# Attention in groups of 256 tokens, uneven FFN blocks and all weight casts on one engine, in a fused attention and FFN kernel

## The chip, the cores and the metric

The kernel runs on one core of one Trainium2 chip. The metric is the device time of one execution in microseconds (us), as the median of several executions. The profile is one execution recorded by the hardware profiler; its span is 1.7 to 2.1 us shorter than the time that is reported for it. Executions are called fast when they lie within 1.5% of the fastest of the same kernel, and only those are compared.

## The reference, cut to what matters

Attention within chunks of 64 tokens for 8 heads of 64, then a feed-forward network (FFN) with a squared Relu:

```python
# q, k, v: (8 batches, 8 heads, 576, 64) float32, each split into chunks of 64 tokens
scores = scale * q_c @ k_c.T
attn = exp(scores - max(scores)) / (sum(...) + 1e-09)
x = (attn @ v_c)                 # as 4608 tokens x 512
h = np.maximum(x @ w_in, 0.0)    # w_in: 512 x 2048
out = (h * h) @ w_out            # w_out: 2048 x 512, out: 4608 x 512 float32
```

## The kernel before

Tokens are handled in nine blocks of 512. The FFN of a block runs on TensorE, and the attention of the next block is laid between its matmuls. The scheduler keeps the program's own order, so the place of a call in the source is its place in each engine's queue. The parts that matter here:

```python
wst_pool = tile_pool(name="wst", bufs=2)          # staging of float32 weights
...
def load_w_in(i):
    ...
    for h in range(2):
        eng = nc.vector if h == 0 else nc.gpsimd  # half of the casts on VectorE
        eng.tensor_copy(out=w_in_bf[...], in_=st[...])
...
def transpose_qk(j, r):
    ps = ps_att.tile([128, 1024], FP32, name="ps_att")
    psb = ps.bitcast(BF16)                        # 2048 bf16 columns
    for which, src in ((0, q_sb), (1, k_sb)):
        ... 8 transposes of src into psb[:, which*1024 : (which+1)*1024]
    for which in range(2):                        # both copies after all 16
        nc.vector.tensor_copy(out=qkT[:, which], in_=psb[:, which * 1024:(which + 1) * 1024])
...
def ffn_in(j):
    for ft in range(n_ft):                        # 16 slices
        ... 4 matmuls into a ps_ffn tile h
        nc.scalar.activation(out=rl, in_=h, func=AF.Relu)
        nc.vector.tensor_tensor(out=gT[:, ft, :], in0=rl, in1=rl, op=ALU.mult)
...
o_sb = ffn_pool.tile([128, d_model], FP32, name="o_sb", bufs=4)   # output staging
```

The matmuls of the FFN therefore depend on two other engines: ScalarE does Relu and frees a ps_ffn tile, VectorE squares it. VectorE also does the copies of the attention.

Some names, for the lines below. Tiles called ps_* lie in PSUM, the memory that TensorE writes its results into; the other tiles lie in SBUF, the on-chip memory that holds inputs and weights. qkT is q and k transposed, xT the attention's result transposed (the input of the first FFN product), rl the Relu, gT its square (the input of the second FFN product), o_sb the output staging. GpSimd casts weights to bf16, SyncE issues the transfers (DMA). A semaphore is a counter that one engine raises and another waits for. In all fences `...` stands for lines that are left out.

The softmax here doesn't subtract the row's maximum and nothing guards it: scores larger than these inputs give would overflow.

## Time and profile before

| | before |
|---|---|
| time, median of 3 executions | 351.23 us |
| span of the profile | 349.6 us |
| first FFN matmul | 58.14 us |
| one block of 512 tokens with attention inside | 32.03 us |

The first 58 us are start-up, the rest is bound by TensorE; the prediction below shows the lines for that. One more line also belongs here, and I did not look at it before I predicted. It is a row of the page's list of costliest groups: line, engine, operation, tiles, count, then busy time and mean ns of one, then the idle time of the engine just before such instructions and who ended it.

```profile
L142 PE MATMUL ps_att<-ident,k_sb 128*128 128x128 bf16 x144 | 12.1, 229 | 0.2 <-DMA k_sb<-in_k_dram 0.2
```

Before all 144 transposes of k together TensorE stood idle for 0.2 us. They follow the transposes of q with nothing between them.

### The profile page before, as it was taken

The numbers are of one execution on the slowest core, as the hardware profiler recorded it, in microseconds if no ns is written. First come the engines' busy times: TensorE is split into PE (matmuls) and PEld (weight loads), VectorE is DVE, ScalarE is ACT, GpSimd is POOL, SyncE is SP. The second block draws the span as 40 slices with busy tenths as digits, with TensorE's granted clock in tenths as the row PEclk, the third lists the DMA queues.
The fourth block names the chain that finished last, engine by engine and source line by source line (L and its number), as shares of the span: only waits on it lengthen the run. The fifth ranks groups of instructions, "written<-read, shape, count | busy, mean of one in ns | idle before, by whom it ended". The sixth has DMA issues, their size and how long they took to land.

```text
span 349.6 us, 6592 instructions
## 1 busy us (share of the span) xinstructions
PE 293.8 (84%) x2693; PEld 149.9 (43%) x2736; DVE 132.1 (38%) x314; ACT 123.0 (35%) x199; POOL 11.6 (3%) x17
## 2 busy tenths in 40 slices
PE   0400026999999999999999999999999999999995
PEld 0300013454554555455445545554554455454442
DVE  0012136343465235615541652356155416522400
ACT  1000020542355137314722551473147225514621
POOL 1024220000000000000000000000000000000000
PEclk9999999999999999999999999999999999999999
DMA  9979689793397249427932971494289220011002
GB/s 173 175 264 348 224 233 181 169 200 80 110 220 134 83 125 198 104 86 162 171 93 80 223 144 68 127 194 104 90 173 175 77 83 9 3 60 62 0 39 81
DMA packets 123165, 46.56 MB, mean 133 GB/s; under 512 B 114432, under 2 KB 114432, under 8 KB 123136
## 3 DMA queue, kind: packets, MB, share of 16 engines
q1 hardware_dynamic: 123136, 46.15, 56.6%
q8 instruction: 21, 0.34, 0.5%
q14 instruction: 8, 0.07, 0.1%
HBM read 36.70 MB, written 9.44 MB: 132 GB/s over the span
## 4 chain that ended last, share of the span: by engine, by line
PE 82%; DMA 7%; SPq 5%; DVE 3%; issue 1%; ACT 0%; POOL 0%
PE ps_ffn L240 36%; PE ps_ffn L260 36%; DMA w_out_st<-in_moe_w_out_dram 5%; PE ps_att L142 4%; PE ps_att L211 3%; SPq L83 2%; DMA w_in_st<-in_moe_w_in_dram 2%; PE ps_att L182 2%; PE ps_att L162 2%; SPq L102 1%; SPq L95 1%; DVE w_out_bf L124 1%; DVE qkT L147 1%; DVE x L193 1%; POOL w_in_bf L114 0%
## 5 line engine op out<-in xcount | busy, mean ns | idle before, releaser
L240 PE MATMUL ps_ffn<-xT,w_in_bf 128*128 128x512 bf16 x552 | 131.8, 385 | 2.9 <-DVE xT L215 1.6
L260 PE MATMUL ps_ffn<-w_out_bf,gT 128*128 128x512 bf16 x557 | 129.1, 379 | 1.1 <-issue 0.2
L246 ACT ACTIVATE rl<-ps_ffn 128x512 bf16<-128x512 f32 x144 | 85.0, 600 | 59.8 <-PE ps_ffn L240 59.8
L247 DVE TENSOR_TENSOR gT<-rl 128x512 bf16<-128x512 bf16 x144 | 60.6, 425 | 95.7 <-ACT rl L246 92.7
L240 PEld LDWEIGHTS <-w_in_bf 128*128 128x128 bf16 x576 | 55.2, 99 | 65.2 <-issue 4.5
L260 PEld LDWEIGHTS <-gT 128*128 128x128 bf16 x576 | 54.8, 98 | 62.5 <-DVE qkT L147 0.3
L252 ACT COPY o_sb<-ps_ffn 128x512 f32<-128x512 f32 x36 | 20.8, 588 | 110.0 <-PE ps_ffn L260 106.7
L162 PE MATMUL ps_att<-qkT 64*64 64x64 bf16 x576 | 7.0, 199 | 35.0 <-DVE qkT L147 35.0
L169 ACT ACTIVATE e<-ps_att 128x1024 bf16<-128x1024 f32 x18 | 17.5, 1023 | 53.2 <-PE ps_att L162 53.2
L215 DVE COPY xT<-ps_att 128x1024 bf16<-128x1024 bf16 x18 | 12.5, 692 | 46.9 <-PE ps_att L211 46.9
L193 DVE TENSOR_TENSOR x<-ps_att,rec 128x256 bf16<-128x256 f32 x72 | 27.2, 419 | 1.2
L147 DVE COPY qkT<-ps_att 128x1024 bf16<-128x1024 bf16 x36 | 23.0, 683 | 1.8 <-PE ps_att L142 1.8
L162 PEld LDWEIGHTS <-qkT 64*64 64x64 bf16 x576 | 5.9, 112 | 38.8 <-DVE qkT L147 35.4
L142 PE MATMUL ps_att<-ident,q_sb 128*128 128x128 bf16 x144 | 12.4, 229 | 10.3 <-DMA q_sb<-in_q_dram 10.2
L142 PEld LDWEIGHTS <-q_sb 128*128 128x128 bf16 x144 | 9.9, 102 | 14.8 <-DMA q_sb<-in_q_dram 11.0
L114 DVE CAST w_in_bf<-w_in_st 128x1024 bf16<-128x1024 f32 x4 | 2.8, 694 | 29.9 <-DMA w_in_st<-in_moe_w_in_dram 29.9
L189 DVE RECIPROCAL rec<-ps_att 128x8 f32<-128x8 f32 x36 | 7.3, 201 | 13.4 <-PE ps_att L182 13.4
L142 PE MATMUL ps_att<-ident,k_sb 128*128 128x128 bf16 x144 | 12.1, 229 | 0.2 <-DMA k_sb<-in_k_dram 0.2
L211 PE MATMUL ps_att<-ident,x 128*128 128x128 bf16 x144 | 11.7, 229 | 0.5 <-DVE x L193 0.5
L211 PEld LDWEIGHTS <-x 128*128 128x128 bf16 x144 | 10.0, 103 | 4.5 <-DVE x L193 0.6
L182 PE MATMUL ps_att<-v_sb,e 64*64 64x65 bf16 x576 | 9.0, 201 | 2.3 <-DVE x L193 1.4
L182 PEld LDWEIGHTS <-e 64*64 64x64 bf16 x576 | 6.6, 111 | 9.5 <-issue 3.8
(13 smaller groups left out, 25.5 us busy)
## 6 DMA issues: line engine op xcount, KB each, us to landing
out_dram<-o_sb SPq DMA_DIRECT2D x36, 256.0 KB, 2.0
q_sb<-in_q_dram SPq DMA_DIRECT2D x32, 256.0 KB, 5.0
k_sb<-in_k_dram SPq DMA_DIRECT2D x32, 256.0 KB, 4.9
v_sb<-in_v_dram SPq DMA_DIRECT2D x80, 64.0 KB, 2.7
v_sb<-in_v_dram SPq DMA_DIRECT2D x32, 128.0 KB, 3.2
w_in_st<-in_moe_w_in_dram SPq DMA_DIRECT2D x4, 1024.0 KB, 5.3
w_out_st<-in_moe_w_out_dram SPq DMA_DIRECT2D x8, 512.0 KB, 4.1
q_sb<-in_q_dram SPq DMA_DIRECT2D x8, 128.0 KB, 4.0
```

Source lines behind the costliest of these rows:

```text
L142: nc.tensor.transpose(out=psb[:, c0:c0 + 128], in_=srcb[:, t, 2 * hp:2 * hp + 2, 1::2], identity=ident)
L147: nc.vector.tensor_copy(out=qkT[:, which], in_=psb[:, which * 1024:(which + 1) * 1024])
L162: nc.tensor.matmul(out=ps[64 * c:64 * c + 64, o0:o0 + 64], lhsT=qkT[64 * a:64 * a + 64, 1, hh, cols], rhs=qkT[64 * a:64 * a + 64, 0, hh, c ...
L169: nc.scalar.activation(out=e.rearrange("p a h t q -> p (a h t q)"), in_=ps, func=AF.Exp, scale=scale)
L182: nc.tensor.matmul(out=ps[64 * p:64 * p + 64, a, hp * (D + 1):(hp + 1) * (D + 1)], lhsT=e[64 * c:64 * c + 64, a, hp % 2, t, :], rhs=vb[64 ...
L193: nc.vector.tensor_tensor(out=x[:, :, a, :], in0=o[:, a, :, 0:D], in1=rec[:, a].to_broadcast([128, n_hp, D]), op=ALU.mult)
L211: nc.tensor.transpose(out=psb[:, c0:c0 + 128], in_=x[:, hp].rearrange("p a d -> p (a d)"), identity=ident)
L240: nc.tensor.matmul(out=h, lhsT=w_in_bf[:, dt, ft * 128:(ft + 1) * 128], rhs=xT[:, dt, :], start=(dt == 0), stop=(dt == n_dt - 1))
L246: nc.scalar.activation(out=rl, in_=h, func=AF.Relu)
L247: nc.vector.tensor_tensor(out=gT[:, ft, :], in0=rl, in1=rl, op=ALU.mult)
L252: nc.scalar.copy(out=o_sb, in_=o_ps)
L260: nc.tensor.matmul(out=o_ps, lhsT=gT[:, ft, tt * 128:(tt + 1) * 128], rhs=w_out_bf[:, ft, :], start=(ft == 0), stop=(ft == n_ft - 1))
```

## The change

The intent is to start the FFN much earlier. The attention is cut into 18 groups of 256 tokens, so that the first xT is ready sooner. VectorE is freed of the weight casts, which had stood ahead of its attention copies; all go to GpSimd. The first FFN block takes three groups (768 tokens), the last takes one (256), so that the start has more work to lay beside the weight loads and the end less to drain. Five staging buffers in place of two, one gT buffer in place of two. Cut to its core:

```diff
-    TCH = 512
+    GT = 256
+    blocks = [[0, 1, 2]] + [[g, g + 1] for g in range(3, n_grp - 1, 2)] + [[n_grp - 1]]
...
-    wst_pool = ctx.enter_context(tc.tile_pool(name="wst", bufs=2))
+    wst_pool = ctx.enter_context(tc.tile_pool(name="wst", bufs=5))
...
-            eng = nc.vector if h == 0 else nc.gpsimd
-            ... eng.tensor_copy(...)
+        nc.gpsimd.tensor_copy(out=w_in_bf[:, :, cols], in_=st)
...
-            for which, src in ((0, q_sb), (1, k_sb)):
-                ... 8 transposes
-            for which in range(2):
-                nc.vector.tensor_copy(
-                    out=qkT[:, which], in_=psb[:, which * 1024:(which + 1) * 1024])
+        for which in range(2):
+            ... 8 transposes
+            dst = qkT[:, which]
+            src = psb[:, which * 1024:(which + 1) * 1024].rearrange("c (h t) -> c h t", h=n_hp)
+            if which == 0:
+                nc.vector.tensor_copy(out=dst, in_=src)
+            else:
+                nc.scalar.copy(out=dst, in_=src)
...
+    load(0)
+    load(1)
+    load_w_in(0)
+    load_w_in(1)
+    load(2)
+    for i in range(2, 8):
+        load_w_in(i)
+    for i in range(8):
+        load_w_out(i)
```

The order of the loads and the slots at which attention is laid between the matmuls (a table called plan) change with it.

## The prediction

> **What bounds the kernel now.** I began with the page's busy shares and its row of tenths. Each slice is 8.74 us.
>
> ```profile
> PE 293.8 (84%) x2693; PEld 149.9 (43%) x2736; DVE 132.1 (38%) x314; ACT 123.0 (35%) x199; POOL 11.6 (3%) x17
> PE   0400026999999999999999999999999999999995
> POOL 1024220000000000000000000000000000000000
> DMA  9979689793397249427932971494289220011002
> ```
>
> TensorE is full from slice 7 to the end and does almost nothing in the first six: the kernel is a start-up of about 58 us and then a TensorE-bound stretch. DMA is busy from the start, but not the bound later. Next I read the timeline of the start.
>
> ```profile
> 12.60 0.40 PE L142 MATMUL ps_att<-ident,k_sb 128*128 128x128 bf16 x2 [0.15 <-DMA k_sb<-in_k_dram]
> ...
> 17.05 10.10 SPq L109 DMA_DIRECT2D w_in_st<-in_moe_w_in_dram  x4
> 22.57 0.69 DVE L114 CAST w_in_bf<-w_in_st 128x1024 bf16<-128x1024 f32 x1 [22.57 <-DMA w_in_st<-in_moe_w_in_dram]
> 22.60 1.56 POOL L114 CAST w_in_bf<-w_in_st 128x1024 bf16<-128x1024 f32 x1 [20.79 <-DMA w_in_st<-in_moe_w_in_dram]
> ...
> 34.69 1.04 POOL L124 CAST w_out_bf<-w_out_st 128x1024 bf16<-128x1024 f32 x1 [1.10 <-DMA w_out_st<-in_moe_w_out_dram]
> ...
> 47.21 0.69 DVE L124 CAST w_out_bf<-w_out_st 128x1024 bf16<-128x1024 f32 x1 [4.09 <-DMA w_out_st<-in_moe_w_out_dram]
> 47.82 2.48 DVE L147 COPY qkT<-ps_att 128x1024 bf16<-128x1024 bf16 x4
> 49.16 0.51 PEld L162 LDWEIGHTS <-qkT 64*64 64x64 bf16 x32 [34.72 <-DVE qkT L147]
> ...
> 58.14 0.59 PE L240 MATMUL ps_ffn<-xT,w_in_bf 128*128 128x512 bf16 x1 [0.78 <-DVE xT L215]
> ```
>
> q and k of the first 512 tokens are there at 12.6 us. Their transposes then lie in PSUM for 34.7 us, because VectorE takes its instructions in order and its share of the weight casts (the last at 47.21) stands ahead of the qkT copies. Those casts come slowly: each pair of staging buffers must be filled and cast before the next transfer is issued. The first FFN matmul is at 58.14.
>
> Last, the chain that ended last, for the price of a steady block and of the end.
>
> ```profile
> 126.22 1.73 PE ps_ffn L240 x8
> ...
> 158.25 1.73 PE ps_ffn L240 x8
> ...
> 318.50 6.69 PE ps_ffn L240 x31
> ...
> 346.16 0.59 ACT o_sb L252
> ```
>
> A block of 512 tokens with the next block's attention inside is 158.25 - 126.22 = 32.03 us. The last one, with none inside, is 346.16 - 318.50 = 27.66, that is 128 matmuls of 0.216 us. So attention of 512 tokens costs TensorE 4.37 us, of a group of 256 tokens 2.18. From 346.16 to the end of the span (349.6) the tail is 3.4 us. The steady part has no slack to give; only the first 58 us have.
>
> **What the Trainium skill says.** (1) "SBUF — State Buffer", section "Who interferes with whom": a VectorE instruction in a two-port mode, or one with two SBUF inputs, and a GpSimd instruction that reads SBUF exclude each other for a whole instruction. The trace agrees as far as it goes: the GpSimd cast that began 0.03 us after a VectorE cast took 1.56 us, the ones alone 1.04 (their access patterns differ too, so this is not proof). The product rl times rl (two SBUF inputs, 425 ns) should meet the casts in the same way. (2) "DMA: Bandwidth & Descriptors", section "Why small descriptors are slow (HBM only)": each packet carries a fixed overhead. Here the 256-byte rows of q, k, v moved at about 211 to 219 GB/s (4 to 13 us), the weights' 2 KB rows at up to 388 (27 to 32 us). (3) "TensorE: Matmul & The Clock Gate", section "What's actually happening": the array runs at half rate until it has been busy for a window of 3.4 us, and falls back after an idle one. In the trace the FFN's weight loads come every 0.43 us from 58.94 to 63.63 and then at 0.21: some 13 slow matmuls, costing 2.8 us once.
>
> **The change part by part.**
>
> *Queue order.* One queue (SyncE) issues every transfer in program order, and the instruction listing of the changed kernel gives: groups 0 and 1, two w_in chunks of 512 KB, group 2, six w_in chunks, eight w_out chunks, groups 3 and 4, groups 5 and 6, and only then the six stores of the first block. Before, 512 tokens of q, k, v took the queue from 0.74 to 17.05, so 8.2 us a group (later, between 46.4 and 65.4 and with more split transfers, 9.5; from 65.4 to 82.7, 8.7). I take 8.2 for groups 0 and 1, 9 for group 2 (split at a batch edge), 8.7 later.
>
> *First attention.* VectorE has no casts any more. Group 0's q and k land at about 7.8 us (before, one 256 KB transfer landed each 1.2 us from 4.21 on). Transposes to 8.7, the k copy now on ScalarE (1.02, as its 128x1024 exp) to 9.8, scores 1.3 at half clock, exp 1.02, values, reciprocal 0.2 and product, x transposes, xT copy 0.7: about 16. The product becomes one instruction of 128x512, estimated at 0.69 us from two of 0.419 less one fixed part of about 0.15. Group 1 follows it in program order, with its transposes at about 16 to 17.3, v landing near 20, the same chain, and xT ready at about 25. FFN starts at 25 instead of 58.1: 33 us sooner. w_in chunks 0 and 1, issued at 17 and 18, are cast by about 24.
>
> *First block, 768 tokens.* Four slices of ft for 512 tokens: 13 slow matmuls and 3 fast, 6.2 us, to 31.2; transposes of group 2, 0.9, to 32.1. w_in chunk 2 is issued after group 2, at about 27.6, lands at 31 and is cast at about 32.2, so there is almost no wait. Twelve further slices, 10.4, and the rest of group 2's attention, 1.9: 44.4. Then 64 matmuls of 256 columns at half of 0.216, 6.9; ScalarE's Relu at 256 columns is about 0.6 - 0.21 = 0.39 for each 0.43 of TensorE, so nearly level: to about 52. w_out: 14 casts of 1.04 (14.6) and the products meanwhile (12 of 0.425 and 16 of about 0.29, 9.7) share one port; 24.3 from 31.2 on is 55.5. The first output tile wants the last w_out chunk at 55, so I give this 1 us. Six output tiles of 16 x 0.216 = 3.45 make 20.7, attention of groups 3 and 4 another 4.4, the last xT copy 0.8: the second block could begin at about 80.
>
> *Stores.* Five staging buffers let w_out's last chunk be issued when the third w_out cast is done, about 46. Groups 3 and 4 take the queue to about 64, 5 and 6 to about 82. The first store lands near 84.5. There are only four o_sb buffers for six output tiles: the fifth copy on ScalarE waits for that store, and every Relu of the next block stands behind it. TensorE can fill the two other ps_ffn buffers (two slices, 1.73 us, to 81.7) and then waits to about 85. I count 3.3 us, so the second block in effect starts at 83.3.
>
> *Rest.* Six blocks of 32.03 (192.2), one with a single group inside (29.85), the last of 256 tokens (7 + 6.9 = 13.9), tail 3.4: 239.3. The single gT buffer costs nothing, since its first new write comes after the last old read in any case. The k copy adds 2 x 1.02 us of ScalarE to a block, into a half where Relu and exp (11.7 of about 17 us) leave room, with four ps_ffn buffers to cover it.
>
> Sum: 83.3 + 239.3 = 322.6 us of span. The span before was 349.6 where the time was 351.2, so 1.6 is added: **324 us**, 7.7% less. Cross-check: 33 us saved at the start, about 6 given back in waits, gives the same.
>
> **Rivals.** *A: no new wait.* If the queue issues faster (8.2 us a group throughout, 2 us less over four groups) or the stores land at once, the wait for o_sb nearly vanishes: 320 or a little under. For it: in the trace before a queue of 64 KB v transfers goes at a steady 0.6 us each, with few waits. Against it: DMA is at 90% and more in the first slices, and the loads between 46 and 65 us needed 9.5 us a group. *B: the first block becomes DMA- and queue-bound.* 10.5 MB of q, k, v and 8 MB of weights stand ahead of the first store. At 9.5 us a group for the last four the store would go out at 85; if the clock also falls back in the wait (3 us idle is near the window of the third skill item) that adds up to 3: 328 to 331. *C: casts become the bound.* If the port is held against GpSimd more than I take (say 2.2 us a cast), w_out is complete only at about 63, TensorE stands for 8 us at the first output tile, and everything behind slips: 331 to 334. For it: VectorE is busy all through this stage; against it: only two products fall into each 1.73 us. *D: the steady blocks lose*, for instance 0.3 us each through ScalarE, 2 us in all.
>
> **Range and chances.** The gain of 33 us at the start rests on one clear wait of 34.7 us, and none of the rivals returns more than about 12 of it. So A is the low end and B or C the high: 317 to 332. Faster by over 2% (under 344.2): 0.97; within 2%: 0.025; slower: 0.005.
>
> **What would show it.** The first FFN input matmul starting at 23 to 27 us; GpSimd casts of w_out of more than 1.04 us where products run; TensorE idle for 2 to 5 us at about 80 to 86 us with ScalarE's output copy waiting for a store's transfer; 32.0 us from block to block afterwards. I am wrong if FFN starts after 30, if TensorE waits for w_in slices or for w_out by more than 3 us, if no wait shows at the first stores, or if a steady block takes more than 32.3.

## The result, and the profile after

| | before | after |
|---|---|---|
| time, median of 4 executions each, same chip | 350.83 us | 352.54 us |
| lowest and highest | 350.21 to 351.24 | 352.24 to 353.04 |
| span of the profile | 349.6 us | 350.2 us |
| first FFN matmul | 58.14 us | 24.57 us |

The ratio is 1.0052, with a 95% interval of 1.0029 to 1.0075: the same within 2%, and if anything slower. Every ratio in this document is the mean time of one kernel's fast runs over that of the kernel before's fast runs in the same rounds, so it is not quite the ratio of the medians quoted. The output was correct here and in every experiment.

The FFN starts 33.6 us earlier, and the kernel ends no earlier. From the page of the changed kernel, the busy shares, then tenths of 8.76 us each:

```profile
PE 303.3 (87%) x2800; PEld 157.9 (45%) x2800; DVE 120.7 (34%) x268; ACT 142.7 (41%) x233; POOL 18.6 (5%) x28
...
PE   2456979989589988998899889988998899899995
POOL 1021681000000000000000000000000000000000
```

TensorE is now half busy in slice 3 and 70% busy or more from slice 5 on, but for slice 11 and the last. But it shows 8s to the end, in a pattern of two 9s and two 8s, where before it showed only 9s: about four slices are one block of 35 us, so every block has an idle part. The casts now lie in slices 3 to 7 of GpSimd. First the start, from the timeline (start, duration, engine, line, operation, tiles, count; in brackets the idle time before it and who ended it):

```profile
24.57 5.83 PE L224 MATMUL ps_ffn<-xT,w_in_bf 128*128 128x512 bf16 x16 [0.78 <-DVE xT L209]
...
34.84 4.27 PE L224 MATMUL ps_ffn<-xT,w_in_bf 128*128 128x512 bf16 x12 [2.07 <-POOL w_in_bf L113]
...
46.46 3.70 DVE L231 TENSOR_TENSOR gT<-rl 128x512 bf16<-128x512 bf16 x4
...
50.83 7.16 PE L224 MATMUL ps_ffn<-xT,w_in_bf 128*128 128x256 bf16 x64 [2.42 <-DVE xT L209]
```

The FFN starts as foreseen. At 34.84 it had waited 2.07 us for a w_in cast, and the next 12 matmuls took 4.27 us, 0.356 each, where 12 at 0.216 would take 2.59. At 50.83 it had waited 2.42 us for an xT copy on VectorE, which stood behind four products that took 0.9 us each. Next the chain that ended last (start, duration, what): the hand-over to the second block, and the block boundaries.

```profile
86.35 2.51 DMA out_dram<-o_sb
88.97 0.59 ACT o_sb L247
...
126.03 1.74 PE ps_ffn L224 x8
...
161.05 1.74 PE ps_ffn L224 x8
...
301.14 1.74 PE ps_ffn L224 x8
...
332.54 6.99 PE ps_ffn L224 x64
...
346.46 0.59 ACT o_sb L247
```

The wait for the stores came, as foreseen: the chain has the sixth output copy waiting for the second store. The fifth, at 88.17, came after 9.46 us without work on ScalarE; the profile puts its release down to TensorE, but in experiment 1 the same copy is put down to the first store. A block is now 161.05 - 126.03 = 35.02 us where it was 32.03. From 126.03 to 301.14 there are five of them, 175.1. The eighth block, with one group inside, is 332.54 - 301.14 = 31.40. The granted clock of TensorE is listed as 1.00 in the steady block before and after, so a lower clock is not the cause.

Where in a block do 3.0 us go? Of the page's list of costly groups, the row that answers to the one shown of before:

```profile
L139 PE MATMUL ps_att<-ident,k_sb 128*128 128x128 bf16 x144 | 12.2, 233 | 23.9 <-DVE qkT L146 23.9
```

The transposes of k do the same work in the same time, but TensorE now stands 23.9 us before them, all of it for the copy of q on VectorE (L146): 18 waits, one a group, the longest 3.5 us. The timeline of a steady block, just after its start at 126.03, shows one:

```profile
127.56 0.43 DVE L231 TENSOR_TENSOR gT<-rl 128x512 bf16<-128x512 bf16 x1 [5.12 <-ACT rl L230]
127.60 0.61 PE L139 MATMUL ps_att<-ident,q_sb 128*128 128x128 bf16 x8
127.80 0.60 ACT L230 ACTIVATE rl<-ps_ffn 128x512 bf16<-128x512 f32 x1 [0.27 <-PE ps_ffn L224]
...
128.43 0.43 DVE L231 TENSOR_TENSOR gT<-rl 128x512 bf16<-128x512 bf16 x1 [0.44 <-ACT rl L230]
...
128.77 0.69 DVE L146 COPY qkT<-ps_att 128x1024 bf16<-128x1024 bf16 x1
...
129.51 0.61 PE L139 MATMUL ps_att<-ident,k_sb 128*128 128x128 bf16 x8 [1.30 <-DVE qkT L146]
...
132.54 0.61 PE L139 MATMUL ps_att<-ident,q_sb 128*128 128x128 bf16 x8
...
134.51 0.61 PE L139 MATMUL ps_att<-ident,k_sb 128*128 128x128 bf16 x8 [1.36 <-DVE qkT L146]
```

Read it upwards from the line of 129.51. The k transposes wait 1.30 us for the q copy. The q copy could have run at 128.21, when the q transposes were done, but VectorE takes its instructions in order, and the product ahead of it had to wait until ScalarE's Relu ended at 128.40. So TensorE stands until Relu, a product and a copy have gone by. The second group of the block has the same wait, of 1.36 us (the last line).

Why must k wait for a copy of q, which lies in other columns? The program's instruction listing shows it. This is the first k transpose of the changed kernel, with the semaphores that it waits for, and the same instruction of the kernel before:

```
after   L139 Matmult ps_att<-ident,k_sb 128x128 [waits DVE_49]
before  L142 Matmult ps_att<-ident,k_sb 128x128
```

In the source the copy of q now stands between the two sets of transposes. Both sets write one PSUM tile, and the copy reads that tile. **Theory (T):** the software tracks the tile as a whole, sees a write after a read, and makes k's transposes wait for VectorE. **Rivals:** (R1) the k copy, moved to ScalarE, holds up Relu and with it TensorE; or (R2) the change's other costs (groups, one gT buffer, late stores) make the steady blocks longer and the wait only shows where TensorE stands for another reason.

### The profile page after: what moved, and what is told of

Same layout as the page of the kernel before. It is cut to its first block, busy times and chain, and to the rows that moved or that the text cites. A ratio compares the mean times of both kernels' runs of the same rounds, so it can differ in the third digit from the quotient of the medians.

```text
span 350.2 us, 6792 instructions
## 1 busy us (share of the span) xinstructions
PE 303.3 (87%) x2800; PEld 157.9 (45%) x2800; DVE 120.7 (34%) x268; ACT 142.7 (41%) x233; POOL 18.6 (5%) x28
## 4 chain that ended last, share of the span: by engine, by line
PE 78%; SPq 8%; DVE 6%; ACT 3%; DMA 2%; issue 1%; POOL 0%; ACTq 0%
PE ps_ffn L240 36%; PE ps_ffn L224 35%; SPq L85 3%; PE ps_att L139 3%; DVE gT L231 3%; DVE qkT L146 3%; ACT rl L230 3%; SPq L104 2%; PE ps_att L205 2%; SPq L97 2%; PE ps_att L179 2%; PE ps_att L160 2%; DMA w_st<-in_moe_w_in_dram 1%; DMA out_dram<-o_sb 1%; SPq L111 1%
## 5 line engine op out<-in xcount | busy, mean ns | idle before, releaser
L224 PE MATMUL ps_ffn<-xT,w_in_bf 128*128 128x512 bf16 (+1 forms) x640 | 137.5, 369 | 6.1 <-DVE xT L209 4.0
L231 DVE TENSOR_TENSOR gT<-rl 128x512 bf16<-128x512 bf16 (+1 forms) x160 | 68.0, 428 | 136.2 <-ACT rl L230 131.6
L230 ACT ACTIVATE rl<-ps_ffn 128x512 bf16<-128x512 f32 (+1 forms) x160 | 87.5, 557 | 45.2 <-PE ps_ffn L224 42.7
L224 PEld LDWEIGHTS <-w_in_bf 128*128 128x128 bf16 x640 | 62.0, 100 | 66.1 <-issue 8.8
L139 PE MATMUL ps_att<-ident,k_sb 128*128 128x128 bf16 x144 | 12.2, 233 | 23.9 <-DVE qkT L146 23.9
L148 ACT COPY qkT<-ps_att 128x1024 bf16<-128x1024 bf16 x18 | 18.2, 1012 | 35.5 <-PE ps_att L139 35.5
L189 DVE TENSOR_TENSOR x<-ps_att,rec 128x512 bf16<-128x512 f32 x36 | 24.9, 692 | 1.2
L139 PEld LDWEIGHTS <-k_sb 128*128 128x128 bf16 x144 | 10.5, 104 | 26.3 <-issue 15.7
L146 DVE COPY qkT<-ps_att 128x1024 bf16<-128x1024 bf16 x18 | 12.3, 686 | 21.4 <-PE ps_att L139 21.4
L113 POOL CAST w_in_bf<-w_st 128x1024 bf16<-128x1024 f32 x8 | 8.8, 1096 | 32.7 <-DMA w_st<-in_moe_w_in_dram 32.7
```

What stands on the lines that cost most here:

```text
L139: nc.tensor.transpose(out=psb[:, c0:c0 + 128], in_=srcb[:, i, 2 * hp:2 * hp + 2, 1::2], identity=ident)
L146: nc.vector.tensor_copy(out=dst, in_=src)
L148: nc.scalar.copy(out=dst, in_=src)
L189: nc.vector.tensor_tensor(out=x.rearrange("p h a d -> p a h d"), in0=o[:, :, :, 0:D], in1=rec.to_broadcast([128, 2, n_hp, D]), op=ALU.mult)
L224: nc.tensor.matmul(out=h[:, 0:n], lhsT=w_in_bf[:, dt, ft * 128:(ft + 1) * 128], rhs=xT[:, dt, c:c + n], start=(dt == 0), stop=(dt == n_dt ...
L230: nc.scalar.activation(out=rl[:, 0:n], in_=h[:, 0:n], func=AF.Relu)
```

## The experiments

Twelve kernels ran. The expectations name runs by their labels: e1 to e4 are experiments 1 to 4 here, e8 is 5, e7 is 6, e5 is 7, e6 is 8, e10 is 9, e12 is 10, e11 is 11 and e13 is 12.

### 1. The copies behind both sets of transposes

```diff
             ... 8 transposes
+        for which in range(2):
             dst = qkT[:, which]
             ... copy
```

> The changed kernel with one edit: both sets of transposes (q, then k) come first and the two qkT copies after them, as in the kernel before. Theory T (shared tile: the k transposes wait for VectorE's copy of q because both lie in one PSUM tile): the 18 waits of the k transposes (23.9 us in all) go, a steady block falls from 35.0 to about 32.1 us, the time from 352.5 to 328-333. Theory R1 (ScalarE, which took over the k copy, is what delays the FFN): blocks stay within 0.5 of 35, time 350-354. Theory R2 (groups of 256 cost TensorE more work): the same, 350-354.

Measured: 331.12 us, ratio 0.9459 (0.9411 to 0.9507). The chain of this kernel, two successive block starts:

```profile
219.05 1.73 PE ps_ffn L225 x8
...
251.08 1.73 PE ps_ffn L225 x8
```

A block is 32.03 us again, to the hundredth what it was before. And its timeline at the same place in a block:

```profile
124.41 0.61 PE L139 MATMUL ps_att<-ident,q_sb 128*128 128x128 bf16 x8
...
124.86 0.61 PE L139 MATMUL ps_att<-ident,k_sb 128*128 128x128 bf16 x8
...
125.58 0.69 DVE L147 COPY qkT<-ps_att 128x1024 bf16<-128x1024 bf16 x1
```

The k transposes follow q's without a wait, and the copy comes after. From the first transpose of q to the first of k it takes 0.45 us here; in the changed kernel it took 1.91 in the first group of the block and 1.97 in the second (132.54 to 134.51). The differences, 1.46 and 1.52, make 2.98, the whole loss of a block. Two lines of order are worth 21 us of 352. Groups of 256, the k copy on ScalarE and the single gT buffer are all still there, so none of them lengthens a steady block.

### 2. The order kept, but q and k each in a PSUM tile of its own

```diff
-        ps = ps_att.tile([128, 1024], FP32, name="ps_att")
-        psb = ps.bitcast(BF16)
         for which in range(2):
+            ps = ps_att.tile([128, 1024], FP32, name="ps_att")
+            psb = ps.bitcast(BF16)
```

> The changed kernel with q and k transposed into two PSUM tiles; the order of all instructions is kept (q transposes, q copy on VectorE, k transposes, k copy on ScalarE). T says the shared tile is the cause and not the order: block about 32.1, time 328-334. A rival of T, that the position of the q copy ahead of the k transposes in the program is itself the harm: no change, 350-354. R1: no change.

Measured: 329.54 us, ratio 0.9422 (0.9397 to 0.9448). Its chain:

```profile
183.73 1.73 PE ps_ffn L224 x8
...
215.77 1.73 PE ps_ffn L224 x8
```

The block is 32.04. Here the q copy is again issued between the two sets of transposes, on the same engine, reading the same number of columns; only the tile is another. So the wait comes from sharing a tile, and not from the copy's being there. That the software tracks the tile as a whole is the reading of this; the runs show no more than that one tile makes the wait and two don't.

### 3. The order kept, and the k copy back on VectorE

```diff
             else:
-                nc.scalar.copy(out=dst, in_=src)
+                nc.vector.tensor_copy(out=dst, in_=src)
```

> The changed kernel with the k copy back on VectorE, all else kept (the q copy still stands between the transposes). R1 (ScalarE's k copy): block falls to about 32-33, time 330-336. T: no change in the k transposes' wait, block 34.5-35.5, time 350-354.

Measured: 351.84 us, ratio 1.0061 (1.0020 to 1.0102). Its chain:

```profile
125.78 1.74 PE ps_ffn L224 x8
...
160.73 1.74 PE ps_ffn L224 x8
```

The block is 34.95, so taking 2 us of copies a block off ScalarE gives next to nothing. The wait of the k transposes stays, 27.7 us in all. The rival that blames ScalarE (R1) falls.

### 4. The kernel before, with only the order changed

```diff
                 ... 8 transposes
-            for which in range(2):
                 nc.vector.tensor_copy(
                     out=qkT[:, which], in_=psb[:, which * 1024:(which + 1) * 1024])
```

> The kernel before with one edit: each qkT copy moved to straight after its own transposes, so the k transposes come after the q copy in the same tile. T: two waits of about 1.3 us and their restarts in each of 8 blocks, block from 32.0 to about 35, time from 351 to 370-376. R1 and R2: no change (within 1%), since ScalarE and the group size are untouched.

Measured: 375.74 us, ratio 1.0740 (1.0708 to 1.0772). Its chain, and the row of its list of waits for the k transposes (total us, times, longest):

```profile
133.17 1.74 PE ps_ffn L239 x8
...
168.13 1.74 PE ps_ffn L239 x8
```

```profile
PE ps_att L142 <- DVE qkT L146: 57.3, 18, 36.2
```

The order alone, without anything else of the change, makes a block 34.96 us. The longest wait, 36.2, is at the start, where the copies stand behind VectorE's casts; it was mostly hidden there, since scores waited for the same copies. The other 17 waits average (57.3 - 36.2) / 17 = 1.24 us. By spans the sum closes: the second block begins at 98.05 where it began at 94.01 (4.0 us), and seven blocks with attention inside lose 2.93 each (20.5), together 24.5, which is 374.1 - 349.6. In the built programs all 18 first k transposes wait for VectorE in the changed kernel and in experiment 4, and none carries a wait in the kernel before and in experiment 1. Experiments 1, 2 and 4 make the cause both necessary and sufficient for the loss in the steady blocks.

### 5. The kernel before, with only the casts moved

This asks which part of the change bought the early start.

```diff
-            eng = nc.vector if h == 0 else nc.gpsimd
+            eng = nc.gpsimd
...
-        eng = nc.vector if i % 2 == 0 else nc.gpsimd
+        eng = nc.gpsimd
```

> The kernel before with one edit: all casts on GpSimd. FFN should start at about 24-26 us instead of 58.1. But q and k of the second block stand in the queue behind all weights, whose two staging buffers let them be done only at about 50 us, so the transposes put into slot 14 of the first block hold TensorE until about 60 us; the second block then starts at about 81 us instead of 94: time 335-341. If nothing holds it there: 318-326.

Measured: 340.76 us, ratio 0.9712 (0.9684 to 0.9741). The FFN starts at 24.65 us, as early as in the changed kernel, still with attention in groups of 512. Its timeline shows why that gains only 10 us:

```profile
53.65 0.37 PE L142 MATMUL ps_att<-ident,q_sb 128*128 128x128 bf16 x2 [14.26 <-DMA q_sb<-in_q_dram]
```

TensorE waits 14.26 us for the second block's q, which stands in the queue behind all the weights. So the early start comes from the casts alone. What the larger first block and the load order add is the work that fills the time until q, k and v of the second block are there.

### 6. Experiment 1, with every other cast on VectorE

```diff
-        nc.gpsimd.tensor_copy(out=w_in_bf[:, :, cols], in_=st)
+        eng = nc.vector if i % 2 == 0 else nc.gpsimd
+        eng.tensor_copy(out=w_in_bf[:, :, cols], in_=st)
```

(and the same in load_w_out)

> e1 with every other weight cast back on VectorE (that part of the change undone alone). Theory: VectorE's order puts the first attention behind its last cast (about 45 us), FFN starts at 55-60 us instead of 24.2, the waits of the start and of the stores vanish, time 343-356. Rival: five staging buffers and smaller chunks let the casts finish early, FFN starts before 40 us and the time stays under 338.

Measured: 360.90 us, ratio 1.0289 (1.0261 to 1.0317), more than I expected. The first scores wait for the copies, and these for the last cast on VectorE at 51.26 (I had put it at about 45):

```profile
53.66 0.64 PE L163 MATMUL ps_att<-qkT 64*64 64x64 bf16 x32 [44.93 <-ACT qkT L151]
```

Mechanism right, size wrong: I had not counted that the two groups' chains then follow one after the other (the second group's scores start at 61.94), so the FFN starts at 67.46, later than in the kernel before. So the rest of the change, with the order of the copies put right but without the move of the casts, loses time.

### 7. Experiment 1 with six output buffers

```diff
-                    o_sb = ffn_pool.tile([128, d_model], FP32, name="o_sb", bufs=4)
+                    o_sb = ffn_pool.tile([128, d_model], FP32, name="o_sb", bufs=6)
```

> e1 (copies after both transposes) with six o_sb buffers instead of four. In e1 TensorE stood idle for 4.59 us before 90.43 us, until ScalarE's fifth output copy had a buffer freed by a store that was queued behind the loads of groups 5 and 6, and some ten matmuls after it ran at half rate (about 2.1 us). Theory S (buffers and store order): both go, time 331 to 323-327. Rival: the loads themselves are late and TensorE waits for k of group 5 or 6 instead; then no more than 2 us is gained.

Measured: 325.68 us, ratio 0.9285 (0.9244 to 0.9326). In experiment 1 the wait for the first store was this one, from its timeline:

```profile
90.43 0.59 PE L225 MATMUL ps_ffn<-xT,w_in_bf 128*128 128x512 bf16 x1 [4.59 <-ACT o_sb L248]
```

Its second block took 122.85 - 83.06 = 39.79 us. With six buffers the wait is gone, and the second block takes 115.86 - 83.67 = 32.19. The block starts, from the chain of experiment 1 and then of this one:

```profile
83.06 1.89 PE ps_ffn L225 x8
...
122.85 1.73 PE ps_ffn L225 x8
```

```profile
83.67 1.89 PE ps_ffn L225 x8
...
115.86 1.73 PE ps_ffn L225 x8
```

So the store wait with what follows it (after the 4.59 us, the matmuls ran at about half rate again) cost 7.6 us in that profile, which was the slowest of experiment 1's four executions. By the ratios (the two ran on different chips) it is 1.7% of 350, some 6 us.

The profile of this run also prices the products rl times rl. Two answers for the same row, first for the stretch from 34 to 46 us, where the casts run, then for 84 to 300 us, where there are none:

```profile
L232 DVE TENSOR_TENSOR gT<-rl 128x512 bf16<-128x512 bf16 x10 | 6.8, 710 | 6.7 <-ACT rl L231 6.7
```

```profile
L232 DVE TENSOR_TENSOR gT<-rl 128x512 bf16<-128x512 bf16 x112 | 47.6, 425 | 84.2 <-ACT rl L231 81.4
```

Beside the casts a product takes 0.71 us on average (1.12 for the three between 46 and 57.6 us), alone 0.425. With the four before 34 us, the 16 products of the first 512 tokens average 0.68.

### 8 to 11. What still costs time in the first block

Four attempts on the start-up's waits. In experiment 8, on top of experiment 1, group 2 is loaded after all of w_in:

```diff
-    load(2)
     for i in range(2, 8):
         load_w_in(i)
+    load(2)
...
-            plan = {3: [(T, 2)], 6: [(SC, 2)], 10: [(AV, 2)], 14: [(XT, 2)],
+            plan = {9: [(T, 2)], 11: [(SC, 2)], 13: [(AV, 2)], 15: [(XT, 2)],
```

> e1 with group 2 loaded after all of w_in and its attention moved to slots 9, 11, 13, 15. In e1 TensorE waited 3.86 us before 34.41 us for the third w_in chunk, which stood in the queue behind group 2, and then ran ten matmuls at half rate (2.1 us). Theory W (queue order): that wait and the slow matmuls go, some 2 us comes back at the xT copy of group 2, time 331 to 326-329. Rival: the GpSimd casts, not the queue, set the pace of w_in; then the waits spread over the slices and the time stays at 329-333.

In experiment 9, on top of experiment 7, the first block's product reads one operand from PSUM, so that only one is in SBUF:

```diff
-                out=gT[:, ft, c:c + n], in0=rl[:, 0:n], in1=rl[:, 0:n], op=ALU.mult)
+                out=gT[:, ft, c:c + n], in0=rl[:, 0:n],
+                in1=(h if j == 0 else rl)[:, 0:n], op=ALU.mult)
```

> e5 with the squared Relu of the first block taken as rl times h, h from PSUM, so that the product has one SBUF input and not two (the result is the same: Relu(h) times h). In e5 the 128x512 products took 0.71 to 1.12 us beside the GpSimd casts and 0.425 us later, and TensorE waited 2.19 us for group 2's xT, whose copy stood behind four such products. Theory L (VectorE and GpSimd exclude each other when the product reads SBUF twice): the products go flat at about 0.69 us, the casts stay at 1.04, the wait for xT falls under 0.5 us, time 325.7 to 321-324. Rival: the products are slow because Relu feeds them late; then nothing changes, 324-327.

In experiment 10, on top of experiment 7, four w_in chunks go ahead of group 2:

```diff
-    load_w_in(1)
+    for i in range(1, 4):
+        load_w_in(i)
     load(2)
-    for i in range(2, 8):
+    for i in range(4, 8):
...
-            plan = {3: [(T, 2)], 6: [(SC, 2)], 10: [(AV, 2)], 14: [(XT, 2)],
+            plan = {5: [(T, 2)], 8: [(SC, 2)], 11: [(AV, 2)], 14: [(XT, 2)],
```

> e5 with four w_in chunks ahead of group 2 instead of two, and group 2's attention in slots 5, 8, 11, 14. Theory W: the wait of 2.79 us (and 0.64) for the third and fourth chunk goes and the clock does not fall back, but the products beside the casts still hold back group 2's xT: time 325.7 to 322-325. Rival: the wait only moves to q and k of group 2, as in e6; no gain, 325-327.

Experiment 11 is 9 and 10 together:

> e10 and e12 together, the candidate for the fastest version: neither the chunk nor the xT wait is left, 318-321.

| | median us | ratio | compare with |
|---|---|---|---|
| 8, group 2 late | 331.81 | 0.9470 (0.9423 to 0.9517) | experiment 1: 0.9459 |
| 9, product from PSUM (five fast executions) | 324.85 | 0.9261 (0.9227 to 0.9295) | experiment 7: 0.9285 |
| 10, four chunks first | 326.97 | 0.9326 (0.9294 to 0.9358) | experiment 7: 0.9285 |
| 11, both | 325.34 | 0.9277 (0.9242 to 0.9312) | experiment 7: 0.9285 |

All four missed what I expected: none is clearly better than the kernel that it was built on. Their times fell where the rivals had put them (8, 9 and 10; experiment 11 had none). In experiment 8 the wait for w_in is gone, and in its place TensorE waits 1.05 us for q of group 2, 1.12 for its k and 1.41 for xT. In experiment 10 it waits 0.75 and 0.99 for q and k, and then 4.29 for the fifth chunk of w_in. In experiment 11 the products behave as I had hoped, none of the 16 longer than 0.69 us although the casts run beside them (line of the groups from 24 to 61 us):

```profile
L232 DVE TENSOR_TENSOR gT<-rl,ps_ffn 128x512 bf16<-128x512 bf16 x16 | 10.7, 685 | 15.8 <-ACT rl L231 15.8
```

but TensorE then waits 5.05 us for the fifth chunk. The hold-up of products by casts is real, but what it costs stays open, because a product with an input in PSUM takes 0.69 us also where no cast runs. From the same run's timeline, the casts before and after, and one of three products between them:

```profile
29.24 1.04 POOL L113 CAST w_in_bf<-w_st 128x1024 bf16<-128x1024 f32 x1 [0.97 <-DMA w_st<-in_moe_w_in_dram]
...
31.50 0.69 DVE L232 TENSOR_TENSOR gT<-rl,ps_ffn 128x512 bf16<-128x512 bf16 x1 [0.49 <-ACT rl L231]
...
39.96 1.04 POOL L113 CAST w_in_bf<-w_st 128x1024 bf16<-128x1024 f32 x1 [9.68 <-DMA w_st<-in_moe_w_in_dram]
```

So these 16 average 0.685 where experiment 7 had 0.68: the edit made the products even, not shorter. In the profiles of the changed kernel and of experiments 7, 8, 10 and 11 the DMA engines are busy for nearly all of the stretch from 24 to 58 us (a share of 0.98 in the changed kernel, where the kernel before had 0.85) and move some 270 to 290 GB/s, and taking away one wait uncovers another for data. I read that as a start that is bound by the transfers; it is argued from these misses, and no run tests it by carrying less data.

One execution of experiment 9, the one that was profiled, took 631.79 us, with every matmul at about half its rate from start to end while the clock is listed as 1.0. The other five lie between 323.95 and 327.01. I have no explanation, and use nothing of that profile.

### 12. Experiment 7 with nine even blocks of 512

```diff
-    blocks = [[0, 1, 2]] + [[g, g + 1] for g in range(3, n_grp - 1, 2)] + [[n_grp - 1]]
+    blocks = [[g, g + 1] for g in range(0, n_grp, 2)]
...
-    load(2)
```

(and a plan for a first block of two groups)

> e5 with nine blocks of 512 tokens as before, that is without the first block of 768 and the last of 256; group 2 is loaded with group 3 after the weights. Theory Q (the start is bound by how fast bytes arrive in the queue's order): FFN starts at 24 as in e5, w_in is never waited for, but the second block's k of group 3 lands only at about 57 us and its transposes hold TensorE for some 7 us, so the second block starts at about 71 with 512 tokens done, where e5 is at 83.7 with 768 done (256 tokens are worth 13.8 + 2.2 = 16 us, so 67.7 would be level): time 326-332. Rival: the block sizes have no part in it, 324-326 as e5.

Measured: 330.76 us, ratio 0.9413 (0.9372 to 0.9453), against 0.9285 for experiment 7. Now w_in is never waited for, but the next group's data come too late: TensorE waits 2.95 us for q at 55.12 and 2.12 us more soon after. The uneven blocks, 768 first and 256 last, with the load order and the plan that go with them, are worth some 1.3%.

## Why the prediction was wrong

The start of the FFN was right: predicted at 25 us (33 sooner), measured at 24.57 (33.6 sooner), and for the reason given; experiment 5 shows that the move of the casts is what does it.

**The step that failed is "Rest. Six blocks of 32.03 (192.2), one with a single group inside (29.85)".** It takes the price of a steady block over from the kernel before. The diff had moved the q copy of transpose_qk between the two sets of transposes, and I noticed only that the k copy went to ScalarE: rival D allowed the steady blocks 0.3 us each, through ScalarE. They lost 2.99 us each, through a wait of TensorE on VectorE that did not exist before. The instruction listing had it in one line; I read the listing for the order of the transfers, and never for what TensorE waits for.

The spans give the sizes. The prediction's span was 322.6; the changed kernel has 350.2, and experiment 1, which differs from it only in the order of the copies, 330.7. (That was the slowest of its four executions, 326.7 to 330.7, so the split below is good to a few us.) So of the 27.6 us by which I missed, 19.5 are the order of the copies: 14.9 in the five steady blocks, 1.5 in the eighth, 2.7 before the second block and 0.5 in it (there most of the k wait coincides with the wait for the store). The list of waits has 23.9 us for it in all.

The other 8.1 us are terms that were mis-sized, and can be read from experiment 1:

- *The first block*, +3.1: the second block begins at 83.06 where I had 80 (my terms as written add up to 78.9). I wrote "there is almost no wait" for w_in; it waited 3.86 us there (2.07 in the changed kernel), and slow matmuls followed. The products take 0.71 to 1.12 us beside the casts, as I suspected. What this costs is not shown, since experiments 9 and 11 did not make them shorter on average. But rival C foresaw w_out complete only at 63 and a wait of 8 us for it; the last cast ended at 54.6 and TensorE never waited for w_out. I put the loss down to rival B, a first block bound by the transfers; that is argued and not tested.
- *The stores*, "I count 3.3 us", +4.5: the second block took 39.79 where 32.03 and 3.3 make 35.33. It was right in mechanism, since the fifth output copy did wait for the first store and six buffers take the wait away. The size was 7.6 by profiles (39.79 against 32.19 in experiment 7) or some 6 by ratios. The first store was issued at 87.26 and not at 82, and the slow matmuls after the wait come on top; I had left those to rival B.
- *The rest*, +0.5: once the order of the copies is undone, the blocks of 32.03, the last block and the tail are as predicted.

Of the signs that I had named, three came true (the FFN's start, casts of w_out of over 1.04 us where products run, up to 1.20, TensorE's wait at the first stores, 3.5 us from 88.1 on, where I had put 2 to 5 us at 80 to 86) and the one that said "I am wrong if a steady block takes more than 32.3" is the one that struck. The best version, experiment 7, takes 325.68 us, 7.2% less than the kernel before; the variants 9 and 11 can't be told from it. That it lies near the predicted 324 us does not make the prediction right: it differs from the change in two edits, it lacks the store wait that the prediction counted, and its start is longer.

## What to carry to other kernels

When a change moves the place of an instruction in a queue, and not only its size, list for every engine what each instruction waits for before and after, and first of all for the engine that is the bound; a copy placed between two writes of one tile turns into a wait of the second write. If the copy should start early, give each half a tile of its own. A gain at the start and a loss of 3 us in each block can cancel to a difference of 0.5%, so read the price of one steady block before you conclude that a change did nothing.

## What the Trainium skill lacked or had wrong

- "PSUM — Partial Sum Buffer", section "PSUM bank collisions raise a hardware error", says that accesses of two engines to different banks run clean. The q half (1024 columns of bf16, 2 KB) and the k half of the tile lie in different banks (the built program places the tile over two), and nothing in these runs contradicts the page; the wait is a semaphore in the program. What I found on no page is that a copy out of one half of a tile makes the next write to its other half wait, though in another bank: here 1.30 and 1.36 us, 2.99 us a block, and nothing with two tiles (32.04 us a block).
- "SBUF — State Buffer", section "Who interferes with whom", was right on the point that the prediction could not prove: the product with two SBUF inputs took 0.71 us on average (later 1.12) beside GpSimd's casts and 0.425 alone, and with one input in PSUM 0.685 throughout, the casts beside it 1.04 each. Experiment 5 also settles the doubt about access patterns: there GpSimd does the same half casts of w_in with nothing on VectorE, and two take 2.02 us (at 23.55), where before one took 1.56 beside a VectorE cast. What the hold-up costs these runs do not show: the product with an input in PSUM takes 0.69 also without casts, so taking the hold-up away this way gained nothing.
- "TensorE: Matmul & The Clock Gate", section "What's actually happening", ties the fall to half rate to an idle window of about 3.4 us. In the changed kernel 12 matmuls took 0.356 us each on average instead of 0.216 after two idle stretches of 1.30 and 2.07 us with 0.6 us of transposes between them; their weight loads come 0.43 us apart only from 36.34 on, 1.5 us after the idle time had ended. The page does not say what a window counts for that is idle only in part; these runs don't settle it.
- None of the pages that I read describes an execution like that of 631.79 us, with matmuls at about half rate throughout and a listed clock of 1.0, beside five of 323.95 to 327.01 of the same program.
